# An attention and feed-forward kernel: centroids copied out of PSUM in one piece, and an order table searched with a charge on crossbar transposes beside casting weight transfers

## The chip, the cores and the metric

The kernel runs on one core of a Trainium2 chip. The metric is the device time of one execution in microseconds (us), and lower is better. Most executions of one kernel lie within about 1% of each other here, so every ratio below uses several runs of both kernels that were taken on the same chip. "Fast" is the undisturbed state of a run; an execution more than 1.5% above the fastest one of its kernel counts as slow and is left out of the ratios.

The engines have short names in the profile: PE is TensorE (PEld its weight loads), DVE is VectorE, ACT is ScalarE, POOL is GpSimd, and SP is SyncE, which issues most transfers. DMA is the hardware that moves data. In a line of the profile "out<-in" gives the tiles, and a bracket at the end gives the idle time before the instruction and what ended it. PSUM is the memory that TensorE writes its results to. The tiles most named are `sc_ps` (scores), `p_sb` (their exps), `x_ps` (attention outputs), `hp` (output of fc1, the matmuls with w_in), `g` (its gelu) and `op` (the matmuls with w_out, also called fc2).

## The reference

The first half is attention over 32 heads (4 batches of 8), 768 tokens and 64 columns each. A query sees only the keys that have the same nearest centroid. The second half is a feed-forward block on the 3072 tokens.

```python
q_assign = argmax(einsum('bhsd,hcd->bhsc', normalize(q), normalize(centroids)))   # 16 centroids
k_assign = argmax(einsum('bhsd,hcd->bhsc', normalize(k), normalize(centroids)))
mask = q_assign[..., :, None] == k_assign[..., None, :]
scores = where(mask, q @ k.T / sqrt(64), -1e9)
x = softmax(scores) @ v                       # then heads side by side: 3072 x 512
out = gelu(x @ w_in) @ w_out                  # 512 x 2048 and 2048 x 512, gelu with erf
```

## The kernel before

The kernel lists all its instructions by name and gives them out in the order of one long table of words. A word can name an engine ("putq11@ACT" lets ScalarE do it). Each engine and each transfer queue gets its work in the order in which the table reaches it, so the table decides what stands behind what on every engine and in every transfer queue. It was found by a search against a model of times.

```python
TABLE = ("zero3 cent dm zero2 ssq ones loadq0 ident loadk0 root ... "   # some 2,060 words
         "... v9 dtr8 hik11 exp6a2 ... w3 sc6b2 exp4b2 dtr9 exp6b2 ... "
         "... fc1_0_3_0 fc1_0_3_1 fc1_0_3_2 fev001 v12 fc1_0_3_3 av4b0 t3_2 asnk8 asnq8 fold8 ... ")
...
    plan.run(TABLE.split())
```

Heads 0 to 7 have q and k transposed on TensorE ("trk", "trq"). From head 8 on a DMA transpose does it ("dtr"): it reads the 16-bit tile `st`, which VectorE, GpSimd and ScalarE have filled ("hik", "lok", "hiq", "loq"), and writes `kqT`. From `kqT` TensorE computes the similarity to the centroids ("asn", tile `asn_ps`), VectorE folds it and finds the best centroid, and its one-hot code goes through another transpose (`ohT`) and is "put" into `kqT` as 16 more rows for the scores.

```python
def dtr():
    nc.sync.dma_start_transpose(
        out=new_T().rearrange("p a n d -> p (a n) d"),
        in_=T["st", i].rearrange("p a n d -> p (a n d)"))
```

The weights arrive as 32-bit and are stored as 16-bit. The transfer does the cast, and GpSimd issues it. There are eight parts: w0 to w3 are w_in, w4 to w7 are w_out.

```python
w_ops[n] = add("POOL", 0.8, due,
               lambda: nc.gpsimd.dma_start(out=dst, in_=src), deps, dma=3.6, name=f"w{n}")
```

The centroids are normalized, split into a high and a low 16-bit half, transposed once on TensorE and copied out of PSUM in three pieces, each waiting for the one before:

```python
nc.tensor.transpose(T["chl"][:, 0:128], cent_hl, ident)
...
c9  = add("ACT", 0.3, -72, lambda: nc.scalar.copy(c_cat[0:D, :, 0, :], cps(0, D, 0)), [c8], name="cc0")
c10 = add("ACT", 0.3, -71, lambda: nc.scalar.copy(c_cat[D:2 * D, :, 0, :], cps(0, D, 0)), [c9], name="cc1")
c11 = add("ACT", 0.3, -70, lambda: nc.scalar.copy(c_cat[0:D, :, 1, :], cps(D, 2 * D, 0)), [c10, o_cz], name="cc2")
```

The softmax here doesn't subtract the row's maximum and nothing guards it: scores larger than these inputs give would overflow.

Of the kernel before, what the change touches and what calls it, by code (L numbers as in the profile page):

```python
# [26 lines left out]
    "zero3 cent dm zero2 ssq ones loadq0 ident loadk0 root eps rnorm exptab cn loadk3 "  # L27
    "hiq0@POOL chi clo hik0 warm256 warm256 warm256 warm256 warm256 warm256 warm256 "
    "warm256 warm256 warm256 warm256 warm256 warm256 warm256 warm256 warm256 warm256 "
    "warm256 warm256 warm256 warm256 ctr loq0 warm256 warm256 warm256 trq0 lok0 loadk1 "  # L30
    "hik3@ACT cc0 lok3@DVE hik1@DVE cc1 warm256 trk0 evq0 cc2 loadq1 evk0 loadk2 loadq3 "
    "lok1@DVE warm256 warm256 warm256 warm256 warm256 trk3 loadv1 hiq1 loadq5 loadv6 "
    "asnk0 loq1@DVE evk3@ACT asnq0 trk1 hik2@POOL amax0 trq1 ge0 warm256 warm256 warm256 "
    "ohtr0 evk1 warm256 asnk1 hiq3@ACT evq1@ACT loadq2 loadk4 asnq1 w0 loadv0 loq3 loadk5 "
    "hiq2@POOL putk0 loadq4 putq0 v1@ACT trq3 warm256 sc0b0 hiq5@ACT loadv2 amax1 ge1 "
    "loq2 lok2@DVE hik4 evq3@ACT sc0a1 exp0b0 ohtr1 asnk3 asnq3 sc0a0 putq1 trk2 exp0a1 "
    "exp0a0 sc0a2 loq5 loadk8 exp0a2 loadq6 putk1 trq2 amax3 evk2 sc0b1 hik5 lok5 w7 trq5 "
    "sc0b2 ge3 evq2 asnk2 exp0b1 v0@DVE asnq2 exp0b2 evq5 amax2 sc1b1 trk5 sc1a1 exp1b1 "
    "loadv4 ge2 av0a0 av0a2 av0a1 hiq4 v2 lok4 loq4 sc1a0 evk5 rec0_0 norm0_0 exp1a1 w2 "
    "ohtr2 exp1a0 putk2 sc1b0 asnk5 exp1b0 av0b0 sc1a2 av0b2 exp1a2 loadq7 av0b1 putk3 "  # L40
    "putq3 sc1b2 exp1b2 rec0_1 putq2 trk4 asnq5 loadk6 sc2a0 exp2a0 trq4 sc3a1 norm0_1 "
    "av1a0 evk4 av1a1 av1a2 exp3a1 hiq7 sc2a2 amax5 exp2a2 evq4 ge5 v4 asnk4 asnq4 hiq6 "
    "w5 rec1_0 sc2a1 exp2a1 norm1_0 av1b0 sc3a2 exp3a2 av1b1 loadk7 w4 av1b2 amax4 hik6 "
    "loadv5 ge4 ohtr4 lok6 sc2b0 rec1_1 norm1_1 loadv3 hik7 trk6 lok7 putq4 sc2b1 exp2b0 "
    "putk5 av2a0 av2a1 putk4 putq5 loadq11 exp2b1 sc3a0 fin000 exp3a0 av2a2 rec2_0 sc4a1 "
    "loq7 exp4a1 evk6 w1 v3 trk7 loadq9 sc4a0 norm2_0 fev000 trq7 exp4a0 av3a0 sc5a0 "
    "exp5a0 evk7 av3a1 evq7 av3a2 loadq8 v6 sc4a2 hik8@DVE loq6 exp4a2 v5 trq6 rec3_0 "
    "hiq11 loadk9 asnk7 evq6 sc2b2 norm3_0 asnq7 exp2b2 amax7 sc3b2 lok8 av4a0 av4a2 "
    "av4a1 loadk10 ge7 sc5b1 exp3b2 asnk6 rec4_0 asnq6 loadv12 hiq8@DVE loq8 norm4_0 "
    "exp5b1 amax6 sc5a2 av2b0 hik9 hiq9 exp5a2 av2b2 sc5a1 ge6 ohtr6 exp5a1 sc3b1 loadv7 "  # L50
    "putk6 av2b1 lok9 rec2_1 sc3b0 exp3b1 putq6 norm2_1 exp3b0 fin010 sc6a0 av5a0 exp6a0 "
    "av5a2 loadq12 t3_3@POOL av5a1 putk7 sc6a1 rec5_0 sc6a2 norm5_0 loadk11 t1_3@POOL "
    "putq7 av3b0 loq9 av3b1 av3b2 rec3_1 exp6a1 fev010 sc7a1 loadv9 v9 dtr8 hik11 exp6a2 "
    "sc7a0 norm3_1 fin011 av6a0 fev011 exp7a1 sc7a2 exp7a0 av6a2 av6a1 sc6b0 exp7a2 "
    "fin020 sc4b0 exp6b0 v7@DVE rec6_0 norm6_0 exp4b0 av7a0 av7a2 fev020 av7a1 loadv13 "
    "rec7_0 sc4b2 w3 sc6b2 exp4b2 dtr9 exp6b2 norm7_0 fin030 sc4b1 exp4b1 fev030 fin001 "
    "fc1_0_3_0 fc1_0_3_1 fc1_0_3_2 fev001 v12 fc1_0_3_3 av4b0 t3_2 asnk8 asnq8 fold8 "
    "av4b1 amax8 ge8 av4b2 fc1_0_1_0 fc1_0_1_1 hik10@ACT fc1_0_1_2 fc1_0_1_3 asnk9 asnq9 "
    "gelu0_3 gelu0_1 t1_2 t2_3@POOL fc1_0_2_0 fc1_0_2_1 fc1_0_2_2 fc1_0_2_3 t2_2 loadk12 "
    "fc1_0_0_0 lok10@DVE fold9 w6 amax9 ge9 loadq10 hiq10@DVE rec4_1 fc1_0_0_1 loq10 "  # L60
    "dtr10 fc1_0_0_2 hik12 gelu0_2 fc1_0_0_3 fc1_0_4_0 fc1_0_4_1 fc1_0_4_2 gelu0_0 "
    "fc1_0_4_3 gelu0_4 fc1_0_6_0 fc1_0_6_1 lok12@DVE fc1_0_6_2 fc1_0_6_3 fc1_0_7_0 "
    "lok11@DVE loadv16 gelu0_6 v13 loq11 fc1_0_7_1 fc1_0_7_2 t4_2@POOL hiq12 norm4_1 "
    "fc1_0_7_3 gelu0_7 fc1_0_5_0 fc1_0_5_1 fc1_0_5_2 ohd8 fc1_0_5_3 gelu0_5 sc5b0 exp5b0 "
    "t3_0 fc2_0_P1_1_0 fc2_0_P1_0_0 fc2_0_P1_0_1 loadk15 loadq13 p10_0 fc2_0_P1_1_1 sc5b2 "
    "t3_1 loadq14 fc2_0_P2_0_0 fc2_0_P2_0_1 exp5b2 sc6b1 asnk10 asnq10 loadv8 sc7b0 av5b0 "
    "av5b1 av5b2 exp6b1 exp7b0 putq8 putk8 c110_0 fold10 loadq15 sc7b1 exp7b1 rec5_1 "
    "norm5_1 fc2_0_P1_2_0 loq12 sc7b2 av6b0 loadk13 av6b1 hiq14 loq14@DVE exp7b2 sc8a0 "
    "exp8a0 av6b2 fc2_0_P1_2_1 loadk14 rec6_1 fin021 sc8b1 norm6_1 av7b0 loadk17 sc8a1 "
    "dtr12 p12_0 fev021@ACT av7b2 exp8b1 hik14 av7b1 rec7_1 exp8a1 norm7_1 fc2_0_P2_2_0 "  # L70
    "sc8b2 exp8b2 fin031 loadv14 fev031 hiq13@DVE amax10 sc8a2 exp8a2 fc2_0_P2_2_1 "
    "loadq20 loq13@DVE t1_0 asnk12 p11_0@ACT fc1_1_1_0 asnq12 ge10 fold12 t4_3@POOL "
    "fc1_1_1_1 hik13@ACT sc8b0 amax12 lok13@DVE putq9 t2_0 fc1_1_1_2 exp8b0 fc1_1_1_3 "
    "ge12 dtr11 fc2_0_P2_1_0 fc2_0_P2_1_1 fc1_1_0_0 fc1_1_0_1 loadv10 dtr13 asnk11 "
    "loadq24 asnq11 fold11 amax11 fc1_1_0_2 fc1_1_0_3 ge11 c111_0 gelu1_1 t1_1@POOL t2_1 "
    "fc1_1_3_0 ohd10 putk9 fc1_1_3_1 fc1_1_3_2 gelu1_0 fc1_1_3_3 c112_0@ACT fc1_1_2_0 "
    "fc1_1_2_1 fc1_1_2_2 loadk20 hiq15@ACT gelu1_3 hik15@ACT fc1_1_2_3 fc1_1_5_0 S1_00 "
    "S2_00 S4_00 fc1_1_5_1 lok15@DVE lok14@DVE gelu1_2 fc1_1_5_2 fc1_1_5_3 gelu1_5 "
    "fc1_1_7_0 fc1_1_7_1 fc1_1_7_2 fc1_1_7_3 putq11@ACT fc1_1_6_0 putq10 S3_00 S1_01 "
    "loadq17 gelu1_7 putk11 v8@DVE S2_01 putk10@ACT fc1_1_6_1 fc1_1_6_2 fc1_1_6_3 gelu1_6 "  # L80
    "loadk19 t4_1 fc1_1_4_0 fc1_1_4_1 fc1_1_4_2 fc1_1_4_3 loadk16 asnk13 loq15@DVE "
    "gelu1_4 sc9b1 asnq13 S1_03 fc2_0_P5_0_0 av8a0 av8b0 dtr14 sc9b0 av8a1 S1_02 "
    "fc2_0_P5_0_1 stc1120 S3_01 S2_03 v16@DVE exp9b1 t4_0@POOL loadq16 fold13 loadv11 "
    "fc2_0_P6_0_0 amax13 exp9b0 ge13 sc9a1 asnk14 av8a2 exp9a1 sc9a0 exp9a0 av8b1 sc9b2 "
    "av8b2 exp9b2 S2_02 sc9a2 asnq14 sc11b1 hiq16@DVE rec8_1 exp9a2 exp11b1 fc2_0_P6_0_1 "
    "ohd12 norm8_1 S3_02 dtr15 S3_03 u20_0 fold14 sc10b1 S4_02 exp10b1 av9a0 av9a2 sc11a1 "
    "exp11a1 v14 av9a1 av9b0 sc10b0 putk13 exp10b0 av9b1 hik16 av9b2 lok16@DVE sc10a1 "
    "exp10a1 fc2_0_P7_0_0 sc10b2 S4_03 exp10b2 hiq17@DVE fc2_0_P7_0_1 loq16 rec9_1 sc10a2 "
    "loadv18 asnk15 exp10a2 v10 asnq15 u30_0 sc10a0 exp10a0 norm9_1 putk12 fc2_0_P4_0_0 "
    "putq13 sc11a0 fc2_0_P4_0_1 p50_0@ACT c210_0 av10a0 S4_01 exp11a0 sc11b2 exp11b2 "  # L90
    "av10b0 stc1110 loq17 loadv15 hik17 putq12 av10a1 av10b2 lok17 loadq18 sc11a2 av10a2 "
    "loadk18 amax14 av10b1 v11 sc13b2 dtr16 hik18@DVE exp11a2 stc1100 exp13b2 loadq19 "
    "fc2_0_P3_0_0 rec10_1 sc11b0 norm10_1 fold15 amax15 ge15 fc2_0_P3_0_1 sc12b2 ge14 "
    "exp11b0 exp12b2 av11a0 c120_0 av11a2 lok18 sc12b0 fc2_0_P6_1_0 dtr17 sc12b1 exp12b0 "
    "exp12b1 fc2_0_P6_1_1 sc12a0 loadk21 u21_0 av11b0 av11b1 asnk16 sc12a1 exp12a0 av11a1 "
    "fc2_0_P5_1_0 sc12a2 hik19@DVE asnq16 c220_0 exp12a1 sc13a2 stc1200 fc2_0_P7_1_0 "
    "exp12a2 av11b2 exp13a2 sc13a0 fc2_0_P7_1_1 sc13b1 hiq18 rec11_1 norm11_1 exp13a0 "
    "fc2_0_P5_1_1 av12a0 exp13b1 av12b0 fold16 sc13b0 p51_0@ACT sc13a1 av12b2 exp13b0 "
    "exp13a1 asnk17 av12a1 u31_0 loq18 av12a2 av12b1 lok19 asnq17 ohd14 putk15 putq14 "
    "putq15 putk14 sc14a1 rec12_1 fc2_0_P4_1_0 sc14a2 exp14a1 hiq19 fc2_0_P3_1_0 sc15a1 "  # L100
    "fc2_0_P4_1_1 norm12_1 loadv22 loq19 c221_0@DVE hiq20 fold17 amax17 exp14a2 exp15a1 "
    "dtr18 ge17 av13a0 dfin10 sc14b0 av13b0 asnk18 loadq21 hik20 lok20@DVE exp14b0 sc14b2 "
    "c211_0 av13a1 dtr19 av13b1 amax16 ge16 stc2100 loq20@DVE av13b2 av13a2 loadq29 "
    "sc14a0 ohd16 hiq21@DVE loadk24 loadk22 hik22 rec13_1 exp14b2 norm13_1 asnq18 fold18 "
# [189 lines left out]
def kernel(  # L294
# [121 lines left out]
    def memsets2():  # L416
        nc.gpsimd.memset(c_cat[D:2 * D, :, 1, :], 0.0)
        for t in oh_solo:
            nc.gpsimd.memset(t[:, :, :, 16:32], 0.0)
# [922 lines left out]
```

## Time and profile before

| | before |
|---|---|
| time, median of 3 runs | 292.73 us (292.63 to 295.0) |
| span of the profiled run | 292.5 us |
| TensorE busy | 284.1 us (97%) |
| TensorE's work at its true pace | about 276 us |
| transposes of heads 8 and 9, issue to landing | 9.5 and 5.8 us |

The prediction below shows the busy shares, TensorE's waits, busy time by stretch and ScalarE's first 45 us. In a time line the columns are start, duration, engine, line, operation, tiles and count.

```profile
44.47 1.46 PE L914 MATMUL hp<-xt,w_in_sb 128*128 128x384 f16 x8
45.77 0.34 PE L811 MATMUL x_ps<-vaug,p_sb 128*128 128x65 f16 x6
45.95 0.46 PE L620 MATMUL asn_ps<-c_cat,kqT 128*128 128x32 f16 x12
```

The transfer queue of SyncE shows the two transposes that feed heads 8 and 9. Here the second column is how long the issue itself held SyncE.

```profile
33.97 4.72 SPq L594 DMA_TRANSPOSE kqT<-st  x1
...
39.49 2.40 SPq L594 DMA_TRANSPOSE kqT<-st  x1
```

They are issued 5.5 us apart and land at 43.5 and 45.3 us.

### The profile page before, as it was taken

To read this page: it belongs to the slowest core of one execution; us is meant where nothing else is said; L and a number is where in the kernel's file an instruction comes from. 1 tells how busy PE (TensorE), PEld (TensorE's weight loads), DVE (VectorE), ACT (ScalarE), POOL (GpSimd) and SP (SyncE) were. 2 spreads that over 40 slices of the span, in tenths; PEclk is the share of its full clock that TensorE was granted. 3 is DMA by queue.
4 is the path that set the end of the run, shared out by engine and by line. 5 is a ranking of instruction groups with operands and counts; after the bars stand their busy time and mean duration, and the time that the engine had idled before them with its cause. 6 is when DMAs were issued, how large, how long until landed. Compare 5 with 4: busy or idle time off the path is not lost.

```text
span 292.5 us, 8304 instructions
## 1 busy us (share of the span) xinstructions
PE 284.1 (97%) x3376; PEld 211.1 (72%) x3376; DVE 193.9 (66%) x481; ACT 235.8 (81%) x331; POOL 123.0 (42%) x160
## 2 busy tenths in 40 slices
PE   7999999999899999999999999999999999999995
PEld 5777766676477787765687777766678788756884
DVE  4988766559799597544269777466055728588753
ACT  4999997799799999967799988966699898499500
POOL 5889771742114703032363230341963320829100
DMA  7999999798949999798358669976102233100023
GB/s 254 235 281 241 265 190 232 181 265 145 213 102 212 177 209 205 153 236 196 86 121 196 129 113 210 204 151 164 30 19 51 63 91 90 56 21 0 18 74 126
DMA packets 81173, 43.88 MB, mean 150 GB/s; under 512 B 58608, under 2 KB 81136, under 8 KB 81136
## 3 DMA queue, kind: packets, MB, share of 16 engines
q1 hardware_dynamic: 76624, 38.94, 58.1%
q0 software_dynamic: 4224, 4.19, 8.9%
q8 instruction: 26, 0.43, 0.6%
q10 hardware_dynamic: 288, 0.23, 0.2%
q14 instruction: 11, 0.09, 0.1%
HBM read 27.30 MB, written 6.29 MB: 115 GB/s over the span
## 4 chain that ended last, share of the span: by engine, by line
PE 74%; DMA 10%; DVE 8%; ACT 6%; issue 2%; SPq 0%; POOL 0%; DVEq 0%
PE op L1229 20%; PE hp L914 19%; PE sc_ps L779 14%; PE x_ps L811 8%; PE fx_ps L1050 6%; DMA ohT<-oh 4%; ACT p_sb L788 4%; DMA kqT<-st 4%; PE asn_ps L620 2%; PE tr_ps L578 1%; DVE kqT L728 1%; DMA k_raw<-in_k_dram 1%; DMA cent_sb<-in_centroids_dram 1%; DVE kqT L719 1%; PE asn_ps L618 1%
## 5 line engine op out<-in xcount | busy, mean ns | idle before, releaser
L788 ACT ACTIVATE p_sb<-sc_ps 128x768 f16<-128x768 f32 x192 | 146.5, 810 | 10.3 <-PE sc_ps L779 7.1
L779 PE MATMUL sc_ps<-kqT 80*128 80x384 f16 x384 | 92.5, 325 | 1.2 <-DVE kqT L728 0.4
L914 PE MATMUL hp<-xt,w_in_sb 128*128 128x384 f16 x384 | 66.1, 326 | 1.2 <-ACT g L927 1.2
L811 PEld LDWEIGHTS <-p_sb 128*128 128x128 f16 x1152 | 48.1, 97 | 11.5 <-DVE x_tok L838 0.8
L1229 PEld LDWEIGHTS <-g 128*128 128x128 f16 x480 | 45.4, 97 | 11.6 <-issue 0.3
L927 ACT ACTIVATE g<-hp 128x768 f16<-128x768 f32 x48 | 38.8, 810 | 18.6 <-PE hp L914 18.0
L914 PEld LDWEIGHTS <-w_in_sb 128*128 128x128 f16 x384 | 36.2, 97 | 24.2 <-issue 1.8
L811 PE MATMUL x_ps<-vaug,p_sb 128*128 128x65 f16 x1152 | 52.4, 193 | 0.4 <-DVE x_tok L838 0.4
L1229 PE MATMUL op<-w_out_sb,g 128*128 128x256 f16 x288 | 38.8, 272 | 0.0
L779 PEld LDWEIGHTS <-kqT 80*128 80x128 f16 x384 | 31.6, 98 | 6.8 <-issue 2.2
L523 POOL TENSOR_TENSOR st<-q_raw,st 128x384 f16<-128x384 f32 x22 | 20.7, 939 | 16.5 <-DVE st L384 8.4
L1229 PE MATMUL op<-w_st,g 128*128 128x256 f16 x192 | 27.4, 272 | 0.1
L384 POOL CAST vaug<-v_raw 128x384 f16<-128x384 f32 x18 | 9.5, 531 | 31.0 <-DMA v_raw<-in_v_dram 22.3
L636 DVE TENSOR_REDUCE asb<-asn_ps 128x192 f32<-128x384 f32 x24 | 13.2, 552 | 12.7 <-PE asn_ps L620 12.5
L1229 PEld LDWEIGHTS <-S 128*128 128x128 f16 x192 | 18.0, 97 | 4.9 <-DVE S L944 0.5
L384 POOL CAST st<-k_raw 128x384 f16<-128x384 f32 x17 | 8.9, 526 | 26.3 <-DMA k_raw<-in_k_dram 23.8
L838 DVE TENSOR_TENSOR x_tok<-x_ps,rec 128x384 f16<-128x384 f32 (+1 forms) x40 | 19.0, 475 | 1.0
L384 DVE COPY p<-op 128x256 f32<-128x256 f32 x15 | 6.3, 420 | 19.0 <-PE op L1229 18.7
L831 DVE RECIPROCAL rec<-x_ps 128x6 f32<-128x6 f32 (+1 forms) x40 | 7.5, 187 | 14.5 <-PE x_ps L811 14.2
L523 POOL TENSOR_TENSOR st<-k_raw,st 128x384 f16<-128x384 f32 x14 | 13.1, 937 | 7.1 <-DVE st L384 4.3
L620 PEld LDWEIGHTS <-kqT 128*128 128x128 f16 x288 | 12.0, 96 | 4.4 <-DMA kqT<-st 1.3
L944 POOL TENSOR_TENSOR S<-S,g 128x768 f16<-128x768 f16 x6 | 9.8, 1640 | 11.4 <-ACT g L927 11.4
(125 smaller groups left out, 419.1 us busy)
## 6 DMA issues: line engine op xcount, KB each, us to landing
q_raw<-in_q_dram SPq DMA_DIRECT2D x32, 192.0 KB, 3.7
v_raw<-in_v_dram SPq DMA_DIRECT2D x32, 192.0 KB, 3.8
out_dram<-c SPq DMA_DIRECT2D x48, 128.0 KB, 1.9
k_raw<-in_k_dram SPq DMA_DIRECT2D x31, 192.0 KB, 3.7
w_in_sb<-in_moe_w_in_dram POOLq DMA_DIRECT2D x4, 512.0 KB, 9.3
w_out_sb<-in_moe_w_out_dram POOLq DMA_DIRECT2D x4, 512.0 KB, 9.2
kqT<-st SPq DMA_TRANSPOSE x24, 4.2
k_raw<-in_k_dram ACTq DMA_DIRECT2D x1, 192.0 KB, 3.5
```

The lines of the kernel that those rows point to most:

```text
L384: engine[eng].tensor_copy(o, i)
L523: engine[eng].tensor_sub(t[:, :, D:2 * D], T[w + "raw", i], t[:, :, 0:D])
L620: nc.tensor.matmul(o, t[:, js], c_cat[:, h].rearrange("p a c -> p (a c)"), start=True, stop=True)
L636: nc.vector.tensor_reduce(out=T["asb", i], in_=T["asn", i].rearrange("p n w (a c) -> p n w c a", a=2), axis=AX.X, op=ALU.add)
L779: nc.tensor.matmul(s_ps[:, e, 0:QB], T["kT", i][0:D + C, c * 128:(c + 1) * 128], T["qT", i][0:D + C, t * QB:(t + 1) * QB], start=True, sto ...
L788: nc.scalar.activation(T["p", i, t][:, 2 * cp:2 * cp + 2, :], T["sc", i, t, cp][:, :, 0:QB], ACT_FN.Exp, bias=0.0, scale=float(scale))
L811: nc.tensor.matmul(o, T["p", i, t][:, ch, jj * 128:(jj + 1) * 128], vaugs[turn("va", i)][:, ch, 0:D + 1], start=(ch == 0), stop=(ch == N - 1))
L838: nc.vector.tensor_tensor(T["xtok", b][:, h // 2, j0:j0 + nn, h % 2 * D:(h % 2 + 1) * D], T["x", key][:, :, 0:D], T["rec", key].to_broadca ...
L914: nc.tensor.matmul(T["hp", hb, fp][:, e, 0:QB], w_in_sb[:, m, f * 128:(f + 1) * 128], T["xt", b][:, m, t * QB:(t + 1) * QB], start=(m == 0 ...
L927: nc.scalar.activation(T["g", hb][:, :, fp, :], T["hp", hb, fp][:, :, 0:QB], ACT_FN.Gelu, bias=0.0, scale=1.0)
L1050: nc.tensor.matmul(o, a[p](m), r[p](m), start=start and m == 0, stop=m == 1, skip_group_check=not start)
L1229: nc.tensor.matmul(T["op", b, key], a()[:, f, j * 128:(j + 1) * 128], w[:, f, :], start=(start and f == 0), stop=(f == NB - 1), skip_group ...
```

## The change

The intent was threefold. The centroids leave PSUM in one copy. The put of q for head 0 is split, so that the first scores can start on its first half. And the whole table was searched again, with a model that charges something for every crossbar transpose (the DMA transposes above) that overlaps a casting weight transfer.

```diff
-    "zero3 cent dm zero2 ssq ones loadq0 ident loadk0 root eps rnorm exptab cn loadk3 "
+    "cent zero3 dm ones loadq0 ident ssq root eps rnorm cn loadk0 exptab hik0 chi loadk1 "
 ... (all words of the table in a new order)
-        nc.tensor.transpose(T["chl"][:, 0:128], cent_hl, ident)
+        for a in range(2):
+            nc.tensor.transpose(T["chl"][:, a * 128:(a + 1) * 128],
+                                cent_hl[:, a].rearrange("p b d -> p (b d)"), ident)
 ... (cc0, cc1, cc2 removed)
+    c11 = add("ACT", 0.4, -72, lambda eng: copy(
+        eng, c_cat, T["chl"][:, 0:256].rearrange("p (a h c) -> p h a c", a=2, h=H)), [c8],
+        name="cc", alt={"DVE": 0.34})
 ...
+            if i == 0:
+                def put_half(t):
+                    nc.vector.tensor_scalar(
+                        T["qT", 0][D:D + C, t * QB:(t + 1) * QB],
+                        T["ohps", 0][0:C, t * QB:(t + 1) * QB], float(VAL), None, op0=ALU.mult)
```

Around the first fc1 block the new table reads as follows (cut):

```text
... loadk14 loadk12 ... loadq12 ... loadq10 ... loadk10 ... loadv7 ... w1 v7 ... w4 ... hik12 ... dtr9 ... dtr8 ... w6 ...
... sc5b2 asnk8 asnq8 fc1_0_3_0 exp5b2 fc1_0_3_1 fc1_0_3_2 fc1_0_3_3 gelu0_3 fold8 t3_2 asnk9 ...
```

## The prediction

> **What bounds the kernel now.** I read the page's busy shares first, then the waits of TensorE, then busy time by stretch, then the time lines of ScalarE and of the DMA transposes.
>
> ```profile
> PE 284.1 (97%) x3376; PEld 211.1 (72%) x3376; DVE 193.9 (66%) x481; ACT 235.8 (81%) x331; POOL 123.0 (42%) x160
> ```
>
> TensorE is busy for 97% of 292.5 us, so at most 8.4 us are plainly idle. The records flatter it, though: a 384-column matmul has a mean of 325 ns, while in the chain that ended last 98 of them in a row took 16.09 us, or 164 ns each. A gap of up to 0.16 us therefore hides inside "busy". I counted the work at the true cadences: 880 matmuls of 384 columns (384 sc_ps, 384 hp, 112 fx_ps) at 0.163 us are 143.4; 672 op at 0.109 (156 took 17.04 us) are 73.2; 1152 x_ps at 0.030 are 34.6; 157 transposes at 0.056 are 8.8; 480 asn_ps at 0.025 are 12.0; 35 warm-up at 0.109 are 3.8. The sum is about 276 us. So 292.5 minus 276 is about 17 us in which TensorE does not work, plus 3.8 us of warm-up that computes nothing.
>
> ```profile
> PE warm_ps L374 <- DVE dm L403: 1.4, 1, 1.4
> PE hp L914 <- ACT g L927: 1.2, 1, 1.2
> PE asn_ps L620 <- DMA kqT<-st: 0.5, 2, 0.3
> PE sc_ps L779 <- ACT p_sb L788: 0.3, 2, 0.2
> PE chl_ps L450 <- DVE cent_hl L444: 0.3, 1, 0.3
> ```
>
> No wait is large: the 1.2 us behind a gelu is the longest in the middle. In the waits of TensorE, DMA transposes of k and q hold it for 0.5 us in all.
>
> ```profile
> 0.00:10.00 10.00, 8.35 (x94) 6.40 (x94) 5.92 (x19) 6.23 (x12) 5.65 (x24) 1.00 0.82 264
> ...
> 30.00:40.00 10.00, 9.58 (x171) 6.91 (x169) 7.32 (x23) 9.56 (x14) 6.74 (x8) 1.00 1.25 252
> 40.00:50.00 10.00, 9.66 (x126) 6.52 (x122) 6.42 (x19) 8.70 (x13) 4.04 (x6) 1.00 1.19 216
> ...
> 70.00:80.00 10.00, 8.81 (x64) 5.21 (x61) 8.25 (x19) 7.97 (x12) 2.49 (x3) 1.00 0.94 206
> 80.00:90.00 10.00, 9.72 (x141) 7.39 (x140) 9.30 (x22) 9.97 (x14) 1.44 (x2) 1.00 0.66 116
> ...
> 280.00:292.50 12.50, 9.41 (x87) 8.20 (x84) 5.65 (x14) 0.00 (x0) 0.73 (x1) 1.00 0.31 105
> ```
>
> The columns are the stretch, then busy us of TensorE, its weight loads, VectorE, ScalarE and GpSimd, granted clock and DMA. TensorE loses 1.65 us in the first 10, 1.2 us at 70 to 80, and 3.1 us at the end, where the last tile is added and stored. From 180 us to the end part it is always full. ScalarE is the tight neighbour early on:
>
> ```profile
> 11.96 1.52 ACT L788 ACTIVATE p_sb<-sc_ps 128x768 f16<-128x768 f32 x2
> 13.68 7.54 ACT L788 ACTIVATE p_sb<-sc_ps 128x768 f16<-128x768 f32 x10 [0.20 <-PE sc_ps L779]
> 21.68 23.44 ACT L788 ACTIVATE p_sb<-sc_ps 128x768 f16<-128x768 f32 x30 [0.47 <-PE sc_ps L779]
> 44.99 0.52 ACT L382 CAST st<-k_raw 128x384 f16<-128x384 f32 x1
> 45.53 1.28 ACT L927 ACT_TABLE_LOAD   x1
> ```
>
> From 11.96 to 45.0 us it runs 42 exps with 0.67 us idle, 0.78 us each. Until the first gelu the end of that row, not TensorE, sets the pace. TensorE starts the first fc1 block at 44.47 us with about 37.0 us of listed work behind it (warm-up included): 7.5 us of the 17 are lost by then, 3.1 at the end, and some 6 in between.
>
> **What the Trainium skill says.** "Perfetto Trace Analysis", Identifying the Most-Contended Engine, says that matmul busy time is a poor measure of how near TensorE is to its limit, since matmuls are pipelined. This trace agrees (325 ns recorded, 164 ns apart), and that is why I counted the work. "TensorE: Matmul & The Clock Gate", Wait — 56ns, not 53.3ns?, gives columns at 2.4 GHz plus 2.5 ns from start to start, and no less than 25 ns: 162.5, 109.2, 29.6 and 55.8 ns for my four widths, and the runs above agree within 1%. The specification table of the same page calls ScalarE's queue a strict FIFO: a copy waiting for a transfer also holds the gelu behind it, which the trace shows at 75.7 us (1.2 us idle for ohT, then TensorE's 1.2 us for the gelu). "DMA: Bandwidth & Descriptors", SWDGE vs HWDGE vs iDMA, says that casting DMAs are generated by GpSimd and transposes by hardware, but that both use the same 16 DMA engines. The trace agrees that they disturb each other: the two kqT transposes issued at 34.0 and 39.5 us, among weight transfers (issued 26.5, 41.5 and 43.8 us, up to 13.3 us to landing), took 9.5 and 5.8 us, while the median of all 24 is 4.2.
>
> **The change, part by part.**
>
> *Centroids.* Three chained copies (0.26 us each, at 5.89, 6.16 and, behind a 0.80 us copy of kqT, 7.46) become one of 256 columns, which I estimate at 0.4 us. A second 128-column transpose costs 0.056 us, the wider cast on VectorE some 0.05. The last copy ended at 7.72, and the first asn_ps started at 7.82, but its other operand, kqT, came out at 7.16 + 0.55 = 7.71. So the copy was not alone on the path: removing it frees nothing by itself. In the new order q's copy out moves off ScalarE, while on VectorE the lo parts of k and q come first: about 5.56 + 0.5 + 0.5 = 6.6, then kqT until 7.2. The first asn_ps gains about 0.5 us.
>
> *Split q put for head 0.* One 0.55 us instruction becomes two of about 0.35, and the first scores wait only for the first: 0.2 us earlier. Together with a longer VectorE queue before it (two kqT copies ahead of the first put, up to 1.1 us), the first exp gains about 0.3 us, not 0.7.
>
> *New order until the first gelu.* TensorE's work is the same list: one transpose more, one warm-up less. On ScalarE the instruction order shows, between the first exp and the first gelu, 43 exps and 3 casts where there were 42 and one. The row then lasts (33.0 / 42) x 43 + 3 x 0.45 = 35.2 us from about 11.65, ending at 46.8, against 45.5. TensorE has about 0.4 us more work done before fc1 starts. Net: about 0.8 us lost.
>
> *The charge.* In the new order the weight transfers are bunched: three are issued close together just before and around the first two transposes, and from the third transpose on there is none left. But the price that it should save was small. The two slow transposes held VectorE 1.3 us (asb) and TensorE hardly: they are within the 0.5 us above, and that 0.5 lies at 90 and 166 us, after transposes of 5.3 and 5.2 us, when every weight had landed (last issue 43.8, plus 9.0). Those ran among loads of q, k and v, which the charge does not touch. I give it 0.3 us.
>
> *New order from the first gelu on.* The 6 us there are many small waits. What is clear from the order is that the costliest trap stays: one put of q is still on ScalarE in the second fc1 block, and between the comparison that frees its transpose and that put there are only 3.6 us of matmuls, where there were 5.2, for a transfer that took 5.1 us there and 3.1 at the median. The next put on ScalarE is gone. In return the tight k and q transposes have more work ahead of them in the stretch of 50 to 100 us (7 us or more instead of 4.7 for head 12). I expect 1.0 us back, no more, since a fresh order brings fresh collisions.
>
> Sum: -0.3 (start) + 0.8 (ScalarE row) - 0.3 (charge) - 1.0 (rest) = -0.8 us, so 292.7 becomes about 291.9. A search is kept, as a rule, when it wins, and I move to 291.5.
>
> **The rivals.**
>
> *The order closes most gaps.* For it: about 10 us in the middle are not forced by TensorE's work. Against it: 3.1 us at the end cannot move, the first 6 us wait for loads and the centroid chain, and 7.5 of the loss come from ScalarE's row of exps, which did not get shorter. If half of the remaining 6 us went and the row cost nothing, 289.
>
> *ScalarE becomes the bound for longer.* For it: the row above, and its strict queue with a put that waits for a transfer. Against it: at 48 to 57 us it idles 0.49 us before each gelu, so it has room in the fc1 blocks. This would give 294.
>
> *Bunched weights arrive late.* Three casting transfers at once took up to 13.3 us; fc1 needs the second part of w_in, and that order leaves about 9 us of matmuls from its issue to its use. For it: the closest pair landed 9.2 and 13.2 us after issue. Against it: the first of a bunch is quick. If it fails, fc1 stands for 2 to 4 us: 295 to 296.
>
> **Range and chances.** The forced part is firm: 276 of work, 1.4 before the first matmul, 3.1 at the end, nearly 281. The rest is 12 us now; I put it at 8 to 14 afterwards, which gives 288.8 to 294.6. Over 2% faster means under 286.9, or half of all that waiting gone: 0.05. Over 2% slower means above 298.6, which needs late weights and a new trap together: 0.03.
>
> **What would show it.** Right: TensorE's busy time within 2 us of 284, the first asn_ps at about 7.3, the first exp at about 11.6, the last exp before the first gelu ending at 46 to 47.5; a wait of gelu or hp behind ohT near 75 us again; kqT transposes still at 5 us or more later than 80 us, among plain loads. Wrong: the row of exps ending before 45, idle of TensorE outside the two ends under 2 us (then I overrated ScalarE's row), or fc1 waiting for w_in_sb (then the bunching decides it).

## The result and the profile after

| | before, same rounds | changed |
|---|---|---|
| time, median of 4 runs | 292.93 us (292.63 to 295.0) | 302.54 us (299.85 to 303.7) |
| ratio of fast runs | 1 | 1.030 (95% interval 1.021 to 1.039) |
| span of the profiled run | 292.5 us | 299.7 us |
| mean granted TensorE clock | 1.000 | 0.989 |

A ratio is the mean time of one kernel's fast runs over that of the other's in the same rounds, so it isn't quite the ratio of the medians. The changed kernel is 3% slower, far outside the predicted range. All four of its runs show a mean clock below 1 (0.989, 0.994, 0.989, 0.989), so what follows is not peculiar to the profiled run.

The busy shares give no hint: TensorE is busy for longer than before (287.0 against 284.1 us).

```profile
PE 287.0 (96%) x3376; PEld 211.6 (71%) x3376; DVE 200.0 (67%) x482; ACT 237.8 (79%) x339; POOL 121.6 (41%) x150
```

Busy time by stretch finds the place at once. The columns are stretch, length and busy us of TensorE (with its count), then its weight loads, VectorE, ScalarE and GpSimd, granted clock, DMA share and GB/s.

```profile
0.00:10.00 10.00, 8.39 (x93) 6.22 (x93) 5.80 (x18) 5.28 (x11) 6.11 (x24) 1.00 0.81 270
30.00:40.00 10.00, 9.39 (x161) 6.64 (x158) 7.62 (x21) 8.89 (x13) 6.11 (x8) 1.00 1.22 218
40.00:50.00 10.00, 5.26 (x78) 3.46 (x77) 2.61 (x9) 7.86 (x10) 2.37 (x4) 0.93 1.37 161
50.00:60.00 10.00, 9.97 (x84) 6.04 (x85) 6.70 (x11) 3.71 (x6) 7.79 (x8) 0.73 0.75 157
70.00:80.00 10.00, 10.00 (x123) 7.48 (x122) 7.47 (x21) 9.10 (x15) 6.52 (x8) 1.00 0.83 199
```

From 40 to 50 us TensorE has 5.26 us of work where before had 9.66. From 50 to 60 us it looks full, but the clock granted there is 0.73. The same stretch of before had clock 1.00:

```profile
50.00:60.00 10.00, 10.00 (x82) 6.92 (x80) 5.84 (x12) 7.52 (x10) 6.46 (x8) 1.00 0.81 181
```

At 70 to 80 us it is full now, where before had 8.81.

To sum this up I used the prediction's own measure: for each matmul the time from its start to the next start, less its true cadence (0.163 us for 384 columns, 0.109 for 256, and so on). What is left over is lost time.

| lost TensorE time, us | 0 to 40 | 40 to 60 | 60 to 100 | 100 to end | sum |
|---|---|---|---|---|---|
| before | 5.3 | 1.0 | 3.3 | 2.9 | 12.5 |
| changed | 6.1 | 8.1 | 0.8 | 4.8 | 19.7 |
| difference | +0.8 | +7.1 | -2.5 | +1.9 | +7.3 |

The spans of the two profiled runs differ by 7.2 us, so this accounts for all of that. The medians differ by 9.6 us; the profiled runs (294.3 and 301.9 us) were a slower one of before and a quicker one of the changed kernel, and no trace shows where the other 2 us go. The waits of TensorE name the cause of the second column (total, number of times, longest):

```profile
PE asn_ps L618 <- DMA kqT<-st: 4.9, 2, 4.3
PE warm_ps L375 <- DVE dm L404: 1.4, 1, 1.4
```

And the time line of TensorE shows both halves of the loss:

```profile
45.26 0.48 PE L786 MATMUL sc_ps<-kqT 80*128 80x384 f16 x2
50.03 0.50 PE L618 MATMUL asn_ps<-c_cat,kqT 128*128 128x32 f16 x12 [4.29 <-DMA kqT<-st]
50.37 2.72 PE L921 MATMUL hp<-xt,w_in_sb 128*128 128x384 f16 x8
...
56.32 1.95 PE L921 MATMUL hp<-xt,w_in_sb 128*128 128x384 f16 x11
```

TensorE stands for 4.29 us in front of head 8's assignment. Then the eight fc1 matmuls take 2.72 us, and at 56.32 eleven of them take 1.95: 0.34 us each against 0.18. Before, eight took 1.46. This is the half clock. The Trainium skill, "TensorE: Matmul & The Clock Gate", What's actually happening, says that an idle window of about 3.4 us puts TensorE at half its clock, and that it needs about as long a busy window to come back. This trace agrees in kind: 4.29 us of standing, then fc1 matmuls 0.32 us apart in place of 0.163. In detail, half the clock was granted from 48.6 us, 2.9 us into the standing, to 55.5 us, 5.4 us after work had resumed; 6.8 us in all. It costs 2.4 us (lost time at 50 to 60 us), so stall and clock together are 6.7 of the 7.1 us.

ScalarE, whose time line answers to the one that the prediction shows, went almost exactly as expected, and then had nothing to do:

```profile
11.65 2.36 ACT L795 ACTIVATE p_sb<-sc_ps 128x768 f16<-128x768 f32 x3 [0.78 <-PE sc_ps L786]
...
39.98 6.63 ACT L795 ACTIVATE p_sb<-sc_ps 128x768 f16<-128x768 f32 x9 [0.41 <-PE sc_ps L786]
46.63 1.28 ACT L934 ACT_TABLE_LOAD   x1
53.13 0.81 ACT L934 ACTIVATE g<-hp 128x768 f16<-128x768 f32 x1 [5.22 <-PE hp L921]
```

The transfer that TensorE waited for stands in the chain that ended last (start, duration, what), and the issues of SyncE show its neighbour:

```profile
37.11 12.88 DMA kqT<-st
```

```profile
32.50 8.59 SPq L592 DMA_TRANSPOSE kqT<-st  x2
41.13 0.62 SPq L491 DMA_DIRECT2D k_raw<-in_k_dram  x1
```

Two transposes stand back to back in SyncE's queue. The first is head 9's, issued at 32.50 and landed at 41.70. Its issue alone took 4.44 us, so head 8's could only go at 37.11, and it landed at 49.99. Casting weight transfers flew beside them from 28.9 us on: w2 until 40.0, w1 from 37.0 to 46.1, w4 from 40.5 to 53.7 and w6 from 41.7 to 56.6. After that, with all weights landed, the next two transposes (issued at 61.0 and 64.6 us) took 3.7 us each; later ones, among plain loads, took 3.6 to 6.6 us.

One can put a number on the charge's aim: for each of the two transposes, add up how long each casting transfer was in flight beside it. Before, with w4 until 35.1, w1 until 39.7, w3 from 41.5 and w6 from 43.8 us, this gives 1.2 + 5.8 + 2.0 beside head 8's and 0.2 + 3.8 + 1.5 beside head 9's, or 14.5 us. In the changed kernel it is 3.3 + 7.5 + 4.7 + 1.2 beside head 9's (the first of them w5, until 35.8) and 2.9 + 9.0 + 9.5 + 8.3 beside head 8's, or 46 us. The order that was searched with a charge on this overlap has three times as much of it in the measured trace. Longer flights make part of that sum themselves; per us of flight it is 2.1 casting transfers against 0.9.

### The profile page after: what moved, and what is told of

It reads as the page before. It is cut to its first block, busy times and chain, and to the rows that moved or that the text cites. A ratio compares the mean times of both kernels' runs of the same rounds, so it can differ in the third digit from the quotient of the medians.

```text
span 299.7 us, 8308 instructions
## 1 busy us (share of the span) xinstructions
PE 287.0 (96%) x3376; PEld 211.6 (71%) x3376; DVE 200.0 (67%) x482; ACT 237.8 (79%) x339; POOL 121.6 (41%) x150
## 4 chain that ended last, share of the span: by engine, by line
PE 74%; DMA 14%; POOL 5%; DVE 3%; issue 2%; ACT 1%; POOLq 0%; SPq 0%
PE op L1236 21%; PE hp L921 20%; PE sc_ps L786 15%; PE x_ps L818 9%; DMA kqT<-st 9%; PE fx_ps L1057 6%; DMA w_out_sb<-in_moe_w_out_dram 4%; POOL st L521 3%; PE asn_ps L618 2%; POOL st L385 1%; DMA cent_sb<-in_centroids_dram 1%; ACT p_sb L795 1%; DVE g L951 0%; ACT L795 0%; POOL vaug L385 0%
## 5 line engine op out<-in xcount | busy, mean ns | idle before, releaser
L921 PE MATMUL hp<-xt,w_in_sb 128*128 128x384 f16 x384 | 68.2, 333 | 0.0
L1236 PEld LDWEIGHTS <-g 128*128 128x128 f16 x480 | 46.0, 97 | 12.6 <-issue 0.3
L1236 PE MATMUL op<-w_out_sb,g 128*128 128x256 f16 x288 | 39.4, 272 | 0.0
L521 POOL TENSOR_TENSOR st<-k_raw,st 128x384 f16<-128x384 f32 x21 | 20.4, 976 | 19.1 <-DVE st L385 16.8
L521 POOL TENSOR_TENSOR st<-q_raw,st 128x384 f16<-128x384 f32 x19 | 18.1, 953 | 16.4 <-DVE st L385 15.8
L1156 POOL TENSOR_TENSOR S<-g 128x768 f16<-128x768 f16 x7 | 11.8, 1696 | 21.7 <-ACT g L934 15.1
L618 PE MATMUL asn_ps<-c_cat,kqT 128*128 128x32 f16 x288 | 13.0, 178 | 4.9 <-DMA kqT<-st 4.9
L385 POOL CAST st<-q_raw 128x384 f16<-128x384 f32 x14 | 7.5, 538 | 20.8 <-DMA kqT<-st 10.4
## 6 DMA issues: line engine op xcount, KB each, us to landing
w_in_sb<-in_moe_w_in_dram POOLq DMA_DIRECT2D x4, 512.0 KB, 10.1
w_out_sb<-in_moe_w_out_dram POOLq DMA_DIRECT2D x4, 512.0 KB, 12.9
```

Source lines behind the costliest of these rows:

```text
L385: engine[eng].tensor_copy(o, i)
L521: engine[eng].tensor_sub(t[:, :, D:2 * D], T[w + "raw", i], t[:, :, 0:D])
L618: nc.tensor.matmul(o, t[:, js], c_cat[:, h].rearrange("p a c -> p (a c)"), start=True, stop=True)
L921: nc.tensor.matmul(T["hp", hb, fp][:, e, 0:QB], w_in_sb[:, m, f * 128:(f + 1) * 128], T["xt", b][:, m, t * QB:(t + 1) * QB], start=(m == 0 ...
L1236: nc.tensor.matmul(T["op", b, key], a()[:, f, j * 128:(j + 1) * 128], w[:, f, :], start=(start and f == 0), stop=(f == NB - 1), skip_group ...
```

## The experiments

All twelve kernels gave correct results. "Before" was timed again beside each group, at medians of 293.6 to 293.9 us. The edits are moves of words in the table of the changed kernel, unless something else is said. The changed kernel itself was not timed again in these groups, and before stood about 1 us lower in its rounds (292.93 us), so a difference of medians to 302.54 us can be off by that much; the ratios to before are the safer measure.

My theory after the trace: the loss is head 8's late transpose and the clock that falls behind it. The transpose is late because it flies among casting transfers, and it hurts because the new order wants it before the first fc1 matmuls. The rivals: the wait is only a symptom and the new code or the rest of the order is slow too; head 8's own position is at fault, not the casts; the plain loads in the queue, not the casts, slow it down.

**Head 8's assignment behind the first fc1 blocks.**

```diff
-  ... asnk8 asnq8 fc1_0_3_0 ... fc1_0_3_3 gelu0_3 fold8 ... asnk9 ... asnq9 ... fold9 ... fin011 ... fc1_0_1_3
+  ... asnk9 asnq9 fc1_0_3_0 ... fc1_0_3_3 gelu0_3 fold9 ... fc1_0_1_3 asnk8 asnq8 fold8 fin011
```

> Same transfers in the same order, but TensorE's assignment of head 8 stands behind two blocks of fc1 instead of in front of the first, and head 9, whose transpose landed at 41.7 us, is assigned in its place. Theory (the gain was eaten by TensorE standing still 4.3 us at head 8's assignment, and by the half clock that followed): the transpose of head 8 still lands near 50 us, TensorE waits for it under 1 us, the granted clock stays 1.00, and the time falls by 6 to 8 us, to about 295. Rival (the loss is spread over the new order, and the stall only shows where it surfaces): the wait moves elsewhere and the time falls by less than 3 us.

It came out at 297.97 us (296.58 to 298.87), ratio 1.014 [1.009, 1.020]. The flights did not get shorter (9.8 and 14.8 us, the second landing at 50.85), but TensorE waited at most 0.4 us for them there and the clock of the traced run stayed at 1.0 (one of the four runs had 0.994). That gives back 4.6 us, less than I expected: lost time at 40 to 60 us falls from 8.1 to 2.6, and the wait for a later transpose, 0.6 us at 134 us in the changed kernel, is 1.5 us here, at 129 us.

**Weights apart from the two transposes.**

```diff
-  ... w2 ... w1 ... w4 ... dtr9 ... dtr8 w6 ... t1_2@POOL
+  ... w2 w1 ... dtr9 ... dtr8 ... t1_2@POOL w4 w6
```

> One casting weight transfer (second part of w_in) goes out earlier, right behind the one before it, and the last two of w_out only after the assignments of heads 8 and 9. Theory (casting transfers slow the two transposes): head 8's transpose takes 6 to 8 us instead of 12.9, TensorE waits less than 1 us at its assignment, the time falls to 294 to 297. Rival (the plain loads in flight slow it, weights do not matter): it still takes 10 us or more and the time stays within 2 us of 302.

It came out at 295.32 us (293.81 to 296.83), ratio 1.008 [1.002, 1.013], clock 1.0. This is 7.2 us less than the changed kernel by the medians, 6.6 by the ratios. Head 8's transpose takes 7.6 us in place of 12.9, and TensorE's time line has only half a microsecond of waiting for it left:

```profile
46.50 0.47 PE L624 MATMUL asn_ps<-c_cat,kqT 128*128 128x32 f16 x12 [0.57 <-DMA kqT<-st]
```

Head 9's transpose takes longer than before the edit (10.65 against 9.2 us), which the casts alone don't explain. I come back to it.

**Head 8's transpose first in the queue.**

```diff
-  ... dtr9 ... dtr8 ...
+  ... dtr8 ... dtr9 ...
```

> Only the two transposes change places in SP's queue: head 8 before head 9. Theory: head 8's lands at about 43 to 45, so its assignment waits little; head 9's takes the long flight and lands near 50, and its assignment, one fc1 piece group later (about 2 us), waits 1.5 to 3 us. Time about 297 to 299. Rival (the slow flight belongs to head 8's data, not to its turn): no change.

It came out at 300.16 us (299.95 without its one slow run), ratio 1.021 [1.015, 1.027] by the fast runs. Head 8's transpose now takes 6.55 us and is ready in time, head 9's takes 15.8, and on TensorE's time line the stall has moved to head 9's assignment:

```profile
52.29 0.34 PE L624 MATMUL asn_ps<-c_cat,kqT 128*128 128x32 f16 x6 [3.67 <-DMA kqT<-st]
```

The slow flight belongs to the second turn in the queue, whichever head stands there. The stall was longer than I had expected.

**Useless work in the stall.** Forty matmuls of 256 columns write into the assignment's own PSUM tile before it is used. They change nothing in the result and keep the clock up.

```diff
+                if i == 8:
+                    for _ in range(40):
+                        nc.tensor.matmul(T["asn", i].rearrange("p n w c -> p (n w c)")[:, 0:256],
+                                         dm[:, 0:128], dm[:, 128:384], start=True, stop=True)
```

> Forty matmuls of 256 columns without use are put on TensorE just before head 8's assignment, into the tile which the assignment then overwrites; they take about 4.4 us, the length of the stall. The stall itself stays. Theory (a stall of over 4 us lets the granted clock fall, which costs about 2.4 us more): granted clock 1.00, hp matmuls at 0.163 us from start to start right after the stall instead of 0.32, time 2 to 3 us under the changed kernel, about 300. Rival (the fall of the clock has another cause): clock stays at 0.99 and the time does not fall.

It came out at 299.07 us (298.73 without its one slow run), ratio 1.017 [1.011, 1.023] by the fast runs, clock 1.0. The flight is unchanged (13.1 us), and TensorE's time line shows the fc1 matmuls behind it at full pace:

```profile
45.56 4.53 PE L612 MATMUL asn_ps<-dm 128*128 128x256 f16 x40
49.92 0.46 PE L623 MATMUL asn_ps<-c_cat,kqT 128*128 128x32 f16 x12
50.23 1.46 PE L926 MATMUL hp<-xt,w_in_sb 128*128 128x384 f16 x8
```

So the half clock had its cause in the standing. In the trace it was worth 2.4 us between 40 and 60 us, as expected. The whole gain is larger (3.8 us by the fast medians, 4.5 by the spans), but the rest of it, 2.1 us of lost time in the trace, lies after 100 us and is not explained by the clock. The waiting itself, over 4 us, is still there.

**The old order with the new code.**

```diff
-  ... cc0 ... cc1 ... cc2 ... putq0 ...        (table of before)
+  ... cc ... puta0 putb0 ...                   (the rest of the table of before unchanged)
```

> The order of the kernel before, with the new centroid code and the split first put alone: this takes the table search out of the change. Theory (these two parts are harmless and worth a few tenths): 0 to 0.6 us faster than before, so within 0.3% of it, the first exp 0 to 0.4 us earlier than 11.96. Rival (the wider transposes and the longer copy, or the extra put, cost the start): slower than before by 0.5 us or more, which the rest of the change would then have inherited.

Five rounds gave 293.31 us (292.52 to 295.1), ratio 0.999 [0.996, 1.002]. The one-piece copy and the split put are neutral. The whole loss is in the order. One expectation missed: the first exp came at 12.04 us, 0.08 us later than before and not earlier.

**The old order with its weights bunched.** In the kernel before, two weight parts are moved back to just in front of head 8's transpose.

```diff
-  ... w4 ... w1 ... v9 dtr8 ...
+  ... v9 w1 w4 dtr8 ...
```

> The kernel before, with two of its casting weight transfers (second part of w_in, first of w_out) taken out of the early stretch and issued just ahead of head 8's transpose: the bunching of the changed kernel in the old order. Theory (casting transfers in flight slow the transposes, and TensorE stands at the assignment): both transposes take 9 to 15 us, TensorE waits 1 to 4 us at head 8's or head 9's assignment, the time rises by 2 to 6 us. Rival (something else in the new order slows them): the transposes stay at 9.5 and 5.8 us and the time at 293.

The fast runs gave 295.2 us at the median, ratio 1.005 [1.001, 1.009], so the loss of 1.6 us is a little below what I expected. The wait did not come where I expected it. In the traced run, which is slow (299.47 us) and can't be compared in time, head 8's transpose was issued before the casts got going and took only 3.8 us with nothing but plain loads in flight. Head 9's took 8.3 us with about three casts beside it. In the list of TensorE's waits it is the weights that come first, and in this trace half the clock was granted from 54.5 to 61.3 us, beginning 2.3 us into that wait:

```profile
PE hp L921 <- DMA w_in_sb<-in_moe_w_in_dram: 3.1, 1, 3.1
```

**Both remedies together.** The edits of the first two experiments.

> The two repairs that helped most, together: weights apart as in the second experiment and head 9 assigned before head 8 as in the first. Theory: nothing is left of the stall, since 0.6 us of waiting at head 8 remained with the weights apart; time 0.5 to 1 us under that run's 295.3, so about 294.5, on a level with before. Rival (the new order is worse elsewhere by over 1 us): it stays at 295 or more.

It came out at 297.15 us, ratio 1.012 [1.009, 1.015]: no better than with the weights apart alone, a miss (the median is 1.8 us higher, but the two intervals overlap). Lost time does not show a gain from moving the assignment as well. Lost time at 40 to 60 us is 2.1 us (weights apart: 2.0), and from 100 us on it is 5.9 instead of 2.5.

**Only the two late w_out parts moved.**

```diff
-  ... w4 ... dtr9 ... dtr8 w6 ... t1_2@POOL
+  ... dtr9 ... dtr8 ... t1_2@POOL w4 w6
```

> Only the last two transfers of w_out wait until after the assignments of heads 8 and 9; the second part of w_in stays where the changed kernel has it, so one casting transfer overlaps head 8's transpose instead of three. If the number of casting transfers in flight sets the flight time: 7 to 9 us for head 8's transpose instead of 12.9, TensorE waits 0 to 1 us, time 295 to 297. If one is as bad as three: still 11 us or more and a wait of 3 us or more. If w_in then lands late for the fifth fc1 block: a wait of hp for w_in_sb, up to 1 us.

It came out at 297.64 us, ratio 1.015 [1.011, 1.020]. With one casting transfer left in flight for most of the time (w1, until 44.1), head 8's transpose took 9.6 us and landed at 45.9, just in time. Lost time at 40 to 60 us is down to 1.3 us. This margin is thin: two of the four runs show a mean clock of 0.989 and 0.994 as the changed kernel does, so the stall may have come back in them. Again a later transpose makes TensorE wait, 1.7 us at 129 us, and from 100 us on 5.7 us are lost.

**The old order with the late puts on VectorE.** The old order has a put on ScalarE that waits for `ohT` and holds a gelu, worth 1.2 to 1.4 us at 77 us. Here the two puts move.

```diff
-  ... putq11@ACT fc1_1_6_0 putq10 ... gelu1_7 putk11 ... putk10@ACT ... gelu1_4 sc9b1 ...
+  ... fc1_1_6_0 putq10 ... gelu1_7 putq11 putk11 ... gelu1_4 putk10 sc9b1 ...
```

> Old order with the new centroid code and the split put, as in the run that came out at 293.3 (ratio 0.999), but the two puts of q and k (heads 11 and 10) that stand on ScalarE inside the second fc1 block go to VectorE, behind the put of q of head 10 that waits there for the same transpose anyway. Theory: the 1.2 to 1.4 us in which the fc1 matmuls wait for a gelu at 77 us come only from the put that holds ScalarE's queue; they vanish, hp waits less than 0.4 us for a gelu there, and the time is 291.8 to 292.6, ratio 0.995 to 0.998. Rival: VectorE, which is held by the same transpose, then gives the wait back in the sums and lo parts behind it: time within 0.4 us of 293.3 and a new wait of TensorE between 77 and 90 us.

It came out at 293.87 us (293.41 to 294.09), ratio 1.000 [0.997, 1.004]. The rival was right on the time (the ratio is 0.1% above that of the old order with the new code). The trap is gone, and TensorE is full at 70 to 80 us, but VectorE behind it is now the tight engine, and TensorE waits for its sums and folds a few microseconds later: 0.4 of the 1.3 us come back at 80 to 90 us. Another 0.5 us is lost before 40 us, where the edit changed nothing, so one trace does not show that VectorE alone gives the gain back. In busy time by stretch TensorE has 9.06 at 80 to 90 us, where before had 9.72, and VectorE 9.56 and 9.64:

```profile
70.00:80.00 10.00, 10.00 (x84) 6.24 (x82) 9.56 (x23) 7.78 (x12) 1.65 (x2) 1.00 0.72 173
80.00:90.00 10.00, 9.06 (x132) 6.88 (x129) 9.64 (x23) 9.62 (x13) 2.06 (x3) 1.00 0.78 168
```

**Weights further apart.** All of w_in is issued by 24 us (one part of w_out stays in second place).

```diff
-  w0 ... w7 ... w3 ... w5 ... w2 ... w1 ... w4 ... w6
+  w0 ... w7 ... w2 ... w3 w1 ... w5 ... t1_2@POOL w4 w6
```

> Changed kernel with the weight transfers in another order: the four parts of w_in take the first slots, so that the last of them is issued at about 24 instead of 37 us, one part of w_out follows at about 29, and the last two parts of w_out stay behind the first sums of w_out as in the run that came out at 295.3. Only one casting transfer is then left beside head 9's transpose and hardly one beside head 8's, with the same plain loads and the same turns in the queue. Theory (casting transfers set the flight): head 8's transpose 4 to 6 us, head 9's 6 to 9 us, no wait of asn_ps for them over 0.3 us, time 294 to 295.5, so no gain beyond the 0.6 us that were left of that wait. Rival (the plain loads, or the turn behind another transpose, set the flight): head 8's at 7 us or more as in the run with the weights apart.

It came out at 295.92 us, ratio 1.007 [1.003, 1.011]: the time is as good as with the weights apart, and no wait for a transpose is left there. But my numbers for the flights were wrong. Head 8's took 7.3 us and head 9's 10.4, as the rival said, although the last cast beside them ended at 42.0 us. Something else than the casts makes part of the flight.

**What the flight consists of.** The landings answer that. In all traces the 190 transfers that SyncE issues land in the order of their issue, without one exception. (The profile assumes that order among transfers of one semaphore. There are eight, and neighbours in the queue never share one, so the order of neighbours is measured.) So a transpose can't land before what stands ahead of it has landed, and its flight contains that. I therefore took the time from the landing of the last load ahead of the two transposes to the landing of the second one:

| kernel | last load ahead landed | second transpose landed | the pair took | part of it with a cast in flight | MB of weights moved in it |
|---|---|---|---|---|---|
| changed | 40.02 | 49.99 | 10.0 | all | 0.85 |
| assignment late | 38.97 | 50.85 | 11.9 | all | 1.21 |
| head 8 first | 37.64 | 52.24 | 14.6 | all | 1.11 |
| stall filled | 39.00 | 49.20 | 10.2 | all | 0.80 |
| w_out late only | 38.95 | 45.91 | 7.0 | 0.74 | 0.52 |
| weights apart | 39.41 | 46.46 | 7.0 | 0.44 | 0.20 |
| both remedies | 39.29 | 45.97 | 6.7 | 0.39 | 0.08 |
| weights further apart | 41.16 | 46.10 | 4.9 | 0.17 | 0.01 |
| before | 40.54 | 45.31 | 4.8 | 0.80 | 0.13 |

In the new order the pair itself takes 5 us with hardly a cast beside it and 10.0 to 14.6 us with one always there. The rest of each flight is queue. The row of before is a warning: there the pair took 4.8 us although a cast was in flight for 0.80 of it, and in the three kernels that start in the old order with the new code it took 4.7 to 5.5 us with 0.81 to 0.85. (In the old order with its weights bunched the first transpose landed before the second was issued, so there is no pair to measure.) A cast in flight need not be moving much. The queue of the casts (packets, MB, share of the DMA engines' time) over the pair's own window, before and then changed:

```profile
q0 software_dynamic: 127, 0.13, 16.3%
...
q0 software_dynamic: 851, 0.85, 64.7%
```

So the bytes that the casts move beside the pair tell the kernels apart better than the time that they are in flight, though not perfectly (0.08 MB beside a pair of 6.7 us, 0.13 beside one of 4.8). This is a correlation: a longer window also lets more bytes through. Why the casts of before moved so little in that window was not tested.

The split of the flight into queue and pair predicts something: with the five loads that stand in front of the transposes moved behind them, the pair should land early although all casts still fly.

**Loads behind the transposes.**

```diff
-  ... loadk14 loadk12 ... loadq12 ... loadq10 ... loadk10 ... w4 ... hik12 ... dtr9 ... dtr8 w6 ...
+  ... w4 ... dtr9 ... dtr8 loadk14 loadk12 loadq12 loadq10 loadk10 ... w6 hik12 ...
```

> Changed kernel with the five loads of k and q that stand in front of the two transposes in SyncE's queue moved right behind them (and one cast of k on GpSimd behind the last weight transfer, so that all three casting transfers stay in flight). It tells apart two parts of the long flight. In the traces so far all 190 transfers of SyncE's queue land in the order of issue, and behind head 9's landing head 8's needed 2.9 us more without casting transfers and 8.1 to 9.1 us with two or three of them. Theory (flight = what is ahead in the queue + own time, the latter stretched by the casts): head 9's flight falls from 9.2 to 4 to 7 us, head 8's is issued and landed earlier, at 43 to 47 instead of 50 us, though still 6 us or more behind head 9's landing; the wait of asn_ps falls from 4.3 to under 1.5 us; 295.5 to 298.5 us. Rival (the casts alone set the landing, whatever is ahead): head 8's still lands at 48 us or later, TensorE stands 3 us or more, 300 us or more.

It came out at 296.19 us (294.65 to 297.32), ratio 1.008 [1.005, 1.012]. The last load ahead landed at 32.78 and the second transpose at 42.86 us: the pair took 10.1 us, just as in the changed kernel, with casts in flight throughout (1.07 MB moved), and the stall is gone. One number missed: head 8's landed 3.9 us behind head 9's, not 6 or more, probably since the casts now stretch head 9's part of the pair. On TensorE's time line head 8's assignment has no bracket any more, and the wait that is left for a transpose is far later, at 129 us:

```profile
46.24 0.45 PE L624 MATMUL asn_ps<-c_cat,kqT 128*128 128x32 f16 x12
...
129.09 0.32 PE L624 MATMUL asn_ps<-c_cat,kqT 128*128 128x32 f16 x6 [1.45 <-DMA kqT<-st]
```

So queue and casts add up, and taking away either of the two is enough to end the stall.

**Old start, new rest.** The table of before up to the fifth gelu of the first fc1 block, then the words of the changed table that are not yet done.

```diff
-  (changed table)
+  (table of before up to gelu0_5) + (words of the changed table not among them, in their order)
```

> The order of before up to the fifth gelu of the first fc1 block (about 54 us), then the order of the changed kernel for everything that is not yet issued; new centroid code and split put. Theory: the loss of the new order lies wholly in 40 to 60 us (7.1 us against before, while 60 to 100 us gained 2.5 and the rest lost 1.9), so this one loses as little as before until 60 us and keeps the gain after it: 291 to 293.5, ratio 0.990 to 1.000, clock 1.0, lost time at 60 to 100 us about 2 us less than before. Rival (the parts of an order only fit their own start: transposes and buffers arrive at other times, and the gain after 60 us was only the slack that the stall had given to everything but TensorE): 294.5 or more, with new waits between 60 and 100 us.

It came out at 294.78 us (293.55 to 295.71), ratio 1.003 [1.000, 1.007]. The time is the rival's (294.5 or more), but its new waits between 60 and 100 us did not come: the gain there is the theory's (lost time 0.8 us against 3.3 before), so it was not a gift of the stall. The seam costs 1.2 us at 50 to 60 us, and 0.7 and 0.9 us more than before are lost at 118 and 170 us. Its busy time by stretch:

```profile
50.00:60.00 10.00, 9.10 (x60) 5.66 (x58) 5.04 (x11) 7.10 (x9) 5.97 (x7) 1.00 0.95 203
...
70.00:80.00 10.00, 10.00 (x76) 6.42 (x75) 8.99 (x21) 8.12 (x13) 0.99 (x1) 1.00 0.81 176
```

None of the twelve beats the kernel before. The best two, the old order with the new code and the same with the puts on VectorE, are equal to it within 0.5%.

## Why the prediction was wrong

**The start and the row of exps: right.** The first assignment came at 7.35 us and the first exp at 11.65 us, as predicted, and the last one before the first gelu ended at 46.6 instead of 46.8. TensorE lost 0.8 us more by 40 us, where the sum has 0.5 net (minus 0.3 for the start, plus 0.8 for the row). The one-piece copy and the split put are worth nothing in the total, as the neutral run with the old order shows; alone they brought neither forward (first assignment at 7.95 us against 7.82 before), so the earlier start belongs to the new order. Of the other signs that it named, TensorE's busy time was 3 us above 284, by the half clock, and no wait behind `ohT` came near 75 us; transposes of 5.2 to 6.6 us after 80 us came as said. (Its range is off by a few tenths: nearly 281 plus 8 to 14 gives 289 to 295.)

**The charge: this step failed.** The prediction says "I give it 0.3 us" and reasons that the price of the overlap was small in the kernel before, so removing it gains little. Two things in it were wrong. First, it saw that the weight transfers are bunched around the two transposes, and drew from it only what becomes of the later transposes. It worked out no new flight for those two, as if it stayed what it had been in the kernel before. Measured, in the order of their turn, they took 9.2 and 12.9 us instead of 9.5 and 5.8. It also read the old flights as the work of the weight transfers, while by the landings 6.6 of the 9.5 us and 4.5 of the 5.8 us passed before the load just ahead had landed. With what the trace now shows, the term is a landing time: the loads ahead landed at 40.0, the pair needs 10 us behind them among casts, which makes 50.0, against a use at 45.7. That is a loss of 4.3 us, and 2.4 more for the clock. Second, the new table puts head 8's assignment in front of the first fc1 matmuls, where before had eight of them, 1.3 us of work, ahead of it. The prediction did not ask what that does when the operand is late. A 0.3 us term was really a loss of 7.1 us between 40 and 60 us.

**The rival of the bunched weights: the right place, the wrong victim.** It asked whether fc1 would stand for late w_in, and named 2 to 4 us. In the changed kernel w_in was in time (46.1 us), and the transposes that flew beside it were not. In the old order with its weights bunched it was as the rival said: 3.1 us of waiting for w_in in the traced run.

**The clock: not in the sum at all.** The prediction used the skill's page on it for cadences only. A stall of 4.3 us brought the half clock and cost 2.4 us more. In the run with only w_out moved, 1.7 us of waiting at 129 us left the clock at 1.0.

**"The costliest trap stays": wrong, in the other direction.** At 70 to 80 us TensorE lost 1.4 us before and nothing after. The term of minus 1.0 us for the rest of the order was the sum of a gain of 2.5 us at 60 to 100 and a loss of 1.9 us later, so it measures minus 0.6. Its size was fair by luck, not for the reason given.

**What stays open.** Every repaired version of the new order still loses 0.7% or more to before, although at 40 to 60 us it is down to 1.3 to 2.6 us of lost time. Four of the six have a wait of 1.1 to 1.7 us for a transpose at 129 us, and most lose about half a microsecond more near 170 us behind a VectorE sum. The first is not because TensorE arrives earlier: in all six it arrives 5.1 to 5.4 us after the issue of that transpose (changed: 5.6). What differs is the flight, 6.4 to 6.9 us in the four and 5.3 and 4.3 in the other two (changed: 6.2), behind the same three loads. With one trace of each kernel it stays open whether the edits or chance make it longer. Nor is it settled why the pair took 10.0 us in one kernel and 14.6 in another with casts throughout. Neither the number of casts in flight nor the rate at which they moved bytes (0.09 and 0.08 MB per us) explains it. What the model charged is not visible in a trace either.

## What to carry to other kernels

Turn the question "how long does this transfer take" into "when does it land": take the landing of what is ahead of it in its queue, add its own time among its neighbours, and compare that with the first use in the new order. That a neighbour is in flight says little of how much it disturbs; the bytes that it moved were the better sign here. A charge on an overlap in a model of times is worth checking against the overlap that the trace then shows, and a wait on TensorE of some 3 us or more (here 3.1, 3.7 and 4.3 us) is to be counted with the slow matmuls behind it. If one wait is removed from a tight order, read the rest of the trace again: here a wait for a later transpose was 0.6 us in the changed kernel and anything from 0 to 1.7 us in the repaired ones.

## What the Trainium skill lacked or had wrong

- "DMA: Bandwidth & Descriptors", Queues, rings and completion order, warns that completion is not first in, first out per issuing engine. As a guarantee that may stand, but in all fourteen traces here the 190 transfers of SyncE landed in the order of issue. For timing, the queue behaved as a strict line: with the load ahead landed at 32.8 instead of 40.0 us, the pair of transposes landed at 42.9 instead of 50.0.
- The same section says that each DMA engine goes round between queues packet by packet. It gives no figure for what a casting stream does to a transpose. Here two transposes of one head each took 4.9 us as a pair while the casts moved 0.01 MB, and 10.0 to 14.6 us while they moved 0.80 to 1.21 MB.
- No page that I found says how much longer the issue of a transpose holds SyncE when other transfers are in flight. With one casting transfer in flight it held it 1.3 us (the one at 52.4 us of the old start with the new rest), in the crowded stretch 1.5 to 5.9 us, so the next transpose is issued late as well. Plain loads are held up too: the issue of two of them took 6.7 us at 22.6 us in the changed kernel.
- "TensorE: Matmul & The Clock Gate", What's actually happening, agrees with the runs in kind: 1.7 us of waiting left the clock at full speed, 3.1 us (old order with bunched weights), 3.7 and 4.3 us halved it, and 40 useless matmuls in the gap kept it up. But the half clock was granted 2.3, 2.9 and 2.9 us after TensorE had stopped (the profile models the ends of matmuls), sooner than the idle window of about 3.4 us, and lasted 6.8, 3.4 and 6.8 us.
